# Lightning attention with mixture of depths: keys transposed into the state banks, wider compares, a reordered step

## The chip, the cores and the metric

The kernel runs on one core of one Trainium2 chip. The metric is the device time of one execution in microseconds (us). Five engines matter: TensorE (PE, with its weight loads listed apart as PEld), VectorE (DVE), ScalarE (ACT), GpSimd (POOL) and SyncE (SP), which issues loads. All data is fp32.

## The reference: what is computed

Attention with a decay per head is computed in blocks of 64 positions with a running state of 64 by 64 per head. Its output, with the heads side by side, is the input x of a layer in which a gate scores every row, and only the 128 best rows of each batch go through two matrix products.

```python
# q, k, v: (4, 8, 768, 64); lam: one decay per head
for b in range(nb):                                   # blocks of 64
    intra = np.einsum('bhic,bhjc->bhij', qb, kb) * Dmask[None]
    intra = np.einsum('bhij,bhjd->bhid', intra, vb)
    inter = np.einsum('bhid,bhde->bhie', qb * lam_pow[None], kv_state)
    out[:, :, sl] = intra + inter
    kb_dec = kb * rev_pow[None]
    kv_state = lam_block[None, :, None, None] * kv_state + np.einsum('bhsd,bhse->bhde', kb_dec, vb)
# x: (4, 768, 512), w1: (512, 1024), w2: (1024, 512), capacity 128
scores = np.einsum('bsd,d->bs', x, w_gate)
out = x.copy()
for b in range(B):
    top_idx = np.argpartition(-scores[b], capacity)[:capacity]
    xe = x[b, top_idx]
    h = np.maximum(xe @ w1, 0.0)
    ye = h @ w2
    g = 1.0 / (1.0 + np.exp(-scores[b, top_idx]))
    out[b, top_idx] = x[b, top_idx] + g[:, None] * ye
```

## The kernel before

The 4 x 768 rows are worked through in 24 tiles of 128 rows, g = 0 to 23, six for each batch. The program order is the order on each engine. A tile goes through these pieces (POOL multiplies, DVE masks and adds, ACT copies out of PSUM):

```python
def keys_decayed(g):        # POOL: kd = keys * powers of lam                      L184
def transposes(g, name, keep):
    t = loaded[g][0 if name == "qT" else 1]
    tp = bank([128, NHP, L], "tp_" + name)          # one of two PSUM banks, pm0 and pm1
    for hp in range(NHP):
        nc.tensor.transpose(tp[:, hp, :], in_=t[:, 2 * hp : 2 * hp + 2, :], identity=ident[:])
    dst = att.tile([128, NHP, L], FP32, name=name)
    nc.scalar.copy(out=dst[:], in_=tp[:])           # L199
    keep[g] = dst
def queries_decayed(g):     # POOL: qs = qT * powers of lam                         L204
def scores(g):              # PE: 16 small matmuls into po                          L217
def masked(g):              # DVE: p = scores * decay mask                          L224
def start_u(g):             # two PSUM tiles of one bank each, one buffer
    us[g] = [ps_u.tile([128, 512], FP32, name=f"pu{c}") for c in range(2)]
def state_products(g):      # PE: keys times values, columns 0 to 255 of pu0, pu1   L240
def decay_state(n):         # POOL: decayed = state * decay                         L250
def next_state(n):          # DVE: state = pu + decayed                             L261
def from_states(g):         # PE: qs times state, into po                           L271
def from_scores(g):         # PE: p times values, into po                           L282
def outputs(g):             # ACT: po to x_b, then one 256 KB store to out
def gate_scores(g):         # DVE: score of each row into sc                        L306
```

The rank of a row is the number of rows that beat it. The scores of a tile are spread along a row by a transpose, into columns 256 to 383 of a state tile, and compared with the scores of all tiles:

```python
def row(g, u, i=0):
    ...
    pb = us.pop(u)[i][:, 256 : 256 + L]
    nc.tensor.transpose(pb, in_=scs[b][:, t : t + 1].broadcast_to([128, 128]), identity=ident[:])   # L326
    nc.scalar.copy(out=rows_[b][:, t * L : (t + 1) * L], in_=pb)                                    # L329
    pbs[g] = pb

def compare(g):
    b, t = divmod(g, NT)
    sc, pb, beaten = scs[b], pbs.pop(g), beatens[b]
    # equal scores count where they stand earlier                                     L339
    nc.vector.scalar_tensor_tensor(out=cmp[:, :L], in0=pb, scalar=sc[:, t : t + 1], in1=not_before[:],
        op0=ALU.is_equal, op1=ALU.mult, accum_out=beaten[:, t, NT : NT + 1])
    for n in range(t):      # the earlier tiles against this one, from PSUM           L345
        nc.vector.tensor_scalar(out=cmp[:, :L], in0=pb, scalar1=sc[:, n : n + 1], ...,
            op0=ALU.is_gt, op1=ALU.add, accum_out=beaten[:, n, t : t + 1])
    # this tile against all up to it, from the copied row                             L350
    nc.vector.tensor_scalar(out=cmp[:, : (t + 1) * L], in0=rows_[b][:, : (t + 1) * L], ...,
        op0=ALU.is_ge, op1=ALU.add, accum_out=beaten[:, t, t : t + 1])
```

When a batch is complete, `ranks` (DVE) and `tokens` (PE, then DVE; L379, L388) make the list of 128 rows. `fetch` gathers them from `out` with an indirect DMA on POOL (L402), `gate` transposes them (L412), sixteen pieces do the products (eight `hidden`, L440, eight `back`, L454), and an indirect DMA scatters the result. The pieces are spread over the steps of the next batch. One step of the main loop:

```python
for g in range(NG):
    # loads for tile g + 6, one eighth of the weights in steps 4 to 11
    if g + 2 < NG:
        decay_state(2 * g + 4)
    for piece in early.pop(g, []):      # fetch, two steps after the end of a batch
        piece()
    from_scores(g)
    outputs(g)
    if g + 1 < NG:
        scores(g + 1); from_states(g + 1); masked(g + 1)
    start_u(g + 2)
    if g + 2 < NG:
        state_products(g + 2)
        next_state(2 * g + 4)
        decay_state(2 * g + 5)
    gate_scores(g)
    if g + 2 < NG:
        next_state(2 * g + 5)
    pieces = later.pop(g, [])
    starts = g in gates
    if starts:
        gates.pop(g)()
    if g + 2 < NG:
        transposes(g + 2, "qT", qTs)
        queries_decayed(g + 2)
    if g + 3 < NG:
        keys_decayed(g + 3)
    if starts and g > 0:
        row(g - 1, g + 2); compare(g - 1)
    in_order(pieces)
    if g + 2 < NG:
        transposes(g + 2, "kT", kTs)
    if not starts and g > 0 and NGR:
        row(g - 1, g + 2); compare(g - 1)
    if g in ranked:
        ranked.pop(g)()
    ...
```

Of the kernel before, what the change touches and what calls it, by code (L numbers as in the profile page):

```python
# [17 lines left out]
def kernel(  # L18
# [172 lines left out]
    def transposes(g, name, keep):  # L191
        t = loaded[g][0 if name == "qT" else 1]
        tp = bank([128, NHP, L], "tp_" + name)
        for hp in range(NHP):
            nc.tensor.transpose(  # L195
                tp[:, hp, :], in_=t[:, 2 * hp : 2 * hp + 2, :], identity=ident[:]
            )
        dst = att.tile([128, NHP, L], FP32, name=name)
        nc.scalar.copy(out=dst[:], in_=tp[:])  # L199
        keep[g] = dst  # L200
# [88 lines left out]
    def outputs(g):  # L289
# [7 lines left out]
        for c in range(2):  # L297
            nc.scalar.copy(out=x_b[half[c], t, :, 1, :], in_=po[half[1 - c], 1])  # L298
        nc.scalar.dma_start(
            out=out[b, t * L : (t + 1) * L, :], in_=x_b[:, t].rearrange("p a b e -> p (a b e)")  # L300
        )

# [13 lines left out]
    rows_, beatens, toks, pbs = {}, {}, {}, {}  # L316

    def row(g, u, i=0):

        b, t = divmod(g, NT)  # L320
        if t == 0:
# [3 lines left out]
        pb = us.pop(u)[i][:, 256 : 256 + L]  # L325
        nc.tensor.transpose(  # L326
            pb, in_=scs[b][:, t : t + 1].broadcast_to([128, 128]), identity=ident[:]
        )
        nc.scalar.copy(out=rows_[b][:, t * L : (t + 1) * L], in_=pb)  # L329
        pbs[g] = pb  # L330
# [3 lines left out]

    def compare(g):
        b, t = divmod(g, NT)
        sc, pb, beaten = scs[b], pbs.pop(g), beatens[b]
        cmp = mod.tile([128, S], BF16, name="cmp")
        nc.vector.scalar_tensor_tensor(  # L339
            out=cmp[:, :L], in0=pb, scalar=sc[:, t : t + 1], in1=not_before[:],  # L340
            op0=ALU.is_equal, op1=ALU.mult, accum_out=beaten[:, t, NT : NT + 1],
        )
        for n in range(t):
            cmp = mod.tile([128, S], BF16, name="cmp")
            nc.vector.tensor_scalar(  # L345
                out=cmp[:, :L], in0=pb, scalar1=sc[:, n : n + 1], scalar2=None,
                op0=ALU.is_gt, op1=ALU.add, accum_out=beaten[:, n, t : t + 1],
            )
        cmp = mod.tile([128, S], BF16, name="cmp")
# [124 lines left out]

    early, gates, later, ranked = {}, {}, {}, {}
    busy_until = [0]

    def put(step, key, piece):  # L480
# [74 lines left out]
    for g in range(NG):  # L555
# [4 lines left out]
        if g + 2 < NG:  # L560
            decay_state(2 * g + 4)
# [73 lines left out]
```

## Time and profile before

| | |
|---|---|
| median of 3 runs | 196.39 us (195.28 to 197.02) |
| the profiled execution | 194.65 us, span from first to last instruction 192.9 us |
| busy share of the span | PE 82%, PEld 65%, DVE 54%, POOL 51%, ACT 34% |
| moved by DMA | 32.26 MB, 80,964 packets, of which 75,680 under 512 bytes |
| mean granted TensorE clock | 0.973 |

The profile is one execution. Its page gives busy time by engine, the span in 40 slices, the DMA queues, the chain of work that ended last, the costliest groups of instructions, and the DMA issues. A row of a group or of a timeline names line, engine, operation, result and operands, and in brackets the idle time of the engine before it and what ended it; "issue" there means that the profile shows nothing the engine waited for. Matmuls overlap, so TensorE's busy share is not its share of full speed: an idle stretch on its timeline says more.

### The profile page before, as it was taken

To read this page: it belongs to the slowest core of one execution; us is meant where nothing else is said; L and a number is where in the kernel's file an instruction comes from. 1 tells how busy PE (TensorE), PEld (TensorE's weight loads), DVE (VectorE), ACT (ScalarE), POOL (GpSimd) and SP (SyncE) were. 2 spreads that over 40 slices of the span, in tenths; PEclk is the share of its full clock that TensorE was granted. 3 is DMA by queue.
4 is the path that set the end of the run, shared out by engine and by line. 5 is a ranking of instruction groups with operands and counts; after the bars stand their busy time and mean duration, and the time that the engine had idled before them with its cause. 6 is when DMAs were issued, how large, how long until landed. Compare 5 with 4: busy or idle time off the path is not lost.

```text
span 192.9 us, 8120 instructions
## 1 busy us (share of the span) xinstructions
PE 157.5 (82%) x3520; PEld 125.3 (65%) x3520; DVE 104.0 (54%) x393; ACT 66.1 (34%) x161; POOL 98.9 (51%) x110
## 2 busy tenths in 40 slices
PE   0896776969777399998888899989699899979980
PEld 0675665757666399896646689876467689439630
DVE  4824353667884653448664564754927678730010
ACT  2234333544443224533314353444234352111100
POOL 3486777476858641773556846458197410130002
PEclk9999998899999859999999999999999999999999
DMA  4999999998999999998999993110103211011001
GB/s 104 221 225 268 230 226 256 223 259 187 254 297 287 302 252 259 271 286 233 232 259 259 250 251 112 59 49 11 58 17 99 109 61 54 0 54 54 3 0 56
DMA packets 80964, 32.26 MB, mean 167 GB/s; under 512 B 75680, under 2 KB 75680, under 8 KB 80928
## 3 DMA queue, kind: packets, MB, share of 16 engines
q1 hardware_dynamic: 76688, 23.34, 54.2%
q10 hardware_dynamic: 3600, 6.30, 8.9%
q0 software_dynamic: 640, 2.10, 3.1%
q8 instruction: 28, 0.46, 0.9%
q14 instruction: 8, 0.07, 0.1%
HBM read 24.38 MB, written 7.34 MB: 164 GB/s over the span
## 4 chain that ended last, share of the span: by engine, by line
PE 51%; issue 16%; DVE 10%; POOL 9%; DMA 7%; ACT 4%; POOLq 1%; SPq 0%; ACTq 0%
PE ph L440 12%; PE py L454 11%; PE pu L240 5%; PE po L217 5%; PE po L271 5%; PE tp_qT L195 4%; PE tp_kT L195 4%; POOL qs L204 4%; DMA xs<-out_dram,tok 3%; PE po L282 3%; POOL kd L184 3%; POOL decayed L250 3%; DMA kn<-in_k_dram 3%; ACT kT L199 2%; DVE cmp L345 2%
## 5 line engine op out<-in xcount | busy, mean ns | idle before, releaser
L250 POOL TENSOR_TENSOR decayed<-state,decay 128x256 f32<-128x256 f32 x40 | 35.4, 884 | 39.0 <-DVE state L261 31.6
L204 POOL TENSOR_TENSOR qs<-qT,qpow 128x512 f32<-128x512 f32 x24 | 30.5, 1269 | 14.4 <-ACT qT L199 8.9
L440 PE MATMUL ph<-xsT,w_sb 128*128 128x128 f32 x256 | 32.6, 286 | 0.9 <-ACT xsT L416 0.7
L440 PEld LDWEIGHTS ph<-xsT,w_sb 128*128 128x128 f32 x256 | 31.2, 200 | 1.7 <-ACT xsT L416 1.5
L199 ACT COPY qT<-tp_qT 128x512 f32<-128x512 f32 x24 | 14.0, 584 | 50.0 <-PE tp_qT L195 46.8
L454 PE MATMUL py<-w_sb,hs 128*128 128x512 f32 x64 | 29.2, 596 | 0.0
L224 DVE TENSOR_TENSOR p<-po,mask 128x512 f32<-128x512 f32 x24 | 16.5, 689 | 19.2 <-PE po L271 19.2
L184 POOL TENSOR_TENSOR kd<-kn,kpow 128x512 f32<-128x512 f32 x24 | 25.1, 1044 | 3.2 <-DMA kn<-in_k_dram 3.1
L261 DVE TENSOR_TENSOR state<-pu,decayed 128x256 f32<-128x256 f32 x40 | 16.8, 421 | 16.9 <-POOL decayed L250 16.3
L240 PE MATMUL pu<-vn,kd 64*64 64x64 f32 x704 | 19.7, 229 | 7.3 <-issue 5.2
L240 PEld LDWEIGHTS pu<-vn,kd 64*64 64x64 f32 x704 | 16.1, 140 | 10.1 <-issue 7.0
L217 PE MATMUL po<-qT,kT 64*64 64x64 f32 x768 | 18.3, 228 | 5.0 <-issue 4.5
L271 PE MATMUL po<-state,qs 64*64 64x64 f32 x704 | 17.3, 225 | 5.9 <-POOL qs L204 3.0
L199 ACT COPY kT<-tp_kT 128x512 f32<-128x512 f32 x24 | 14.1, 587 | 23.3 <-PE tp_kT L195 23.3
L195 PE MATMUL tp_qT<-ident,qn 128*128 128x128 f32 x96 | 17.4, 309 | 5.1 <-DMA qn<-in_q_dram 5.1
L339 DVE SCALAR_TENSOR_TENSOR cmp<-pu,sc,not_before 128x128 bf16<-128x128 f32 x24 | 8.4, 349 | 23.8 <-ACT sc_row L329 17.0
L217 PEld LDWEIGHTS po<-qT,kT 64*64 64x64 f32 x768 | 14.5, 137 | 8.1 <-issue 5.4
L271 PEld LDWEIGHTS po<-state,qs 64*64 64x64 f32 x704 | 14.5, 138 | 7.1 <-POOL qs L204 3.7
L454 PEld LDWEIGHTS py<-w_sb,hs 128*128 128x128 f32 x64 | 11.5, 190 | 11.0 <-issue 11.0
L345 DVE TENSOR_SCALAR_CACHE_REDUCE cmp<-pu,sc 128x128 bf16<-128x128 f32 x60 | 17.8, 347 | 0.0
L298 ACT COPY x_b<-po 64x256 f32<-64x256 f32 x48 | 17.6, 366 | 0.6
L282 PE MATMUL po<-vn,p 64*64 64x64 f32 x768 | 16.8, 224 | 0.3 <-DVE p L224 0.3
(55 smaller groups left out, 170.6 us busy)
## 6 DMA issues: line engine op xcount, KB each, us to landing
qn<-in_q_dram SPq DMA_DIRECT2D x24, 256.0 KB, 5.3
kn<-in_k_dram SPq DMA_DIRECT2D x24, 256.0 KB, 5.5
vn<-in_v_dram SPq DMA_DIRECT2D x24, 256.0 KB, 6.0
out_dram<-x_b ACTq DMA_DIRECT2D x24, 256.0 KB, 3.6
w_sb<-in_moe_w_dram SPq DMA_DIRECT2D x8, 512.0 KB, 5.9
wg_b<-in_moe_w_gate_dram SPq DMA_DIRECT2D x1, 256.0 KB
xs<-out_dram,tok POOLq DMA_INDIRECT x4, 4.3
out_dram<-y,tok POOLq DMA_INDIRECT x4, 3.1
```

Of the source, the lines that this page charges most:

```text
L184: nc.gpsimd.tensor_tensor(out=kd[:], in0=loaded[g][1][:], in1=kpow[:].rearrange("p a b -> p (a b)").unsqueeze(2).broadcast_to([128, H, D]) ...
L195: nc.tensor.transpose(tp[:, hp, :], in_=t[:, 2 * hp : 2 * hp + 2, :], identity=ident[:])
L199: nc.scalar.copy(out=dst[:], in_=tp[:])
L204: nc.gpsimd.tensor_tensor(out=qs[:], in0=qTs[g][:], in1=qpow[:].rearrange("p a c i -> p a (c i)"), op=ALU.mult)
L217: nc.tensor.matmul(po[half[c], hh, 1, hp, :], lhsT=kT[half[hh], hp, half[c]], rhs=qT[half[hh], hp, half[c]], start=True, stop=True, skip_g ...
L240: nc.tensor.matmul(us[g][c][half[hh], hp * D : (hp + 1) * D], lhsT=kd[half[c], h, :], rhs=vn[half[c], h, :], start=True, stop=True, skip_g ...
L250: nc.gpsimd.tensor_tensor(out=t[:], in0=states[n][:], in1=decay[:], op=ALU.mult)
L271: nc.tensor.matmul(pos[g][half[hh ^ c], hh, 0, hp, :], lhsT=qs[half[hh], hp, half[c]], rhs=states[n][half[hh], hp, :], start=(hp == 0), st ...
L282: nc.tensor.matmul(pos[g][half[hh ^ c], hh, 0, hp, :], lhsT=p[half[c], hh, hp, :], rhs=vn[half[c], 2 * hp + hh, :], start=(hp == 0 and (2 ...
L345: nc.vector.tensor_scalar(out=cmp[:, :L], in0=pb, scalar1=sc[:, n : n + 1], scalar2=None, op0=ALU.is_gt, op1=ALU.add, accum_out=beaten[:, ...
L440: nc.tensor.matmul(ph[:, fc % 4, :], lhsT=w1_sb[:, dc, fc * 128 : (fc + 1) * 128], rhs=keep["xsT"][:, dc, :], start=(dc == 0), stop=(dc == ...
L454: nc.tensor.matmul(py[:], lhsT=keep["hs"][:, fc, :], rhs=w2_sb[:, fc, :], start=(fc == 0), stop=(fc == NFC - 1),)
```

## The change

It does seven things.

1. The transposed keys no longer take one of the two shared banks: they go into columns 256 to 511 of the two state tiles, two pairs of heads in each, directly behind the transposed queries. ACT copies them out in two halves.
2. The row of scores takes a shared bank. Only the compare for equality reads it there; all others read the row that ACT has copied to SBUF, and several are put together: earlier tiles are compared with two or three later ones at once, after tiles 2, 4 and 5 of a batch.
3. The equality compare stands before the second state of the step, the other compares after it.
4. The decayed keys stand at the head of the step, and the decayed queries ahead of the decay of the second state on POOL.
5. The rows of an expert are fetched in the step before, behind the list of rows; the ranks come ahead of the list, in the same step.
6. The six stores of the second batch are held back and written as two stores of three tiles in steps 12 and 13.
7. In the last steps, one expert piece instead of two is in step 23, so that five pieces instead of four stand behind the last fetch.

The core of the diff:

```diff
-    def transposes(g, name, keep):
-        t = loaded[g][0 if name == "qT" else 1]
-        tp = bank([128, NHP, L], "tp_" + name)
...
+    def transposes(g):
+        tq = bank([128, NHP, L], "tq")
+        tk = [u[:, NHP * D :].rearrange("p (a i) -> p a i", i=L) for u in us[g]]
+        W = NHP // 2
+        for i, dst in ((0, tq), (1, None)):
+            for hp in range(NHP):
+                nc.tensor.transpose(
+                    dst[:, hp, :] if i == 0 else tk[hp // W][:, hp % W, :],
+                    in_=loaded[g][i][:, 2 * hp : 2 * hp + 2, :], identity=ident[:],
+                )
+        qT = att.tile([128, NHP, L], FP32, name="qT")
+        nc.scalar.copy(out=qT[:], in_=tq[:])
+        kT = att.tile([128, NHP, L], FP32, name="kT")
+        for i in range(2):
+            nc.scalar.copy(out=kT[:, i * W : (i + 1) * W, :], in_=tk[i])
...
+        if b == 1 and B > 2:
+            kept.append(t)
+        else:
+            store(b, t, t + 1)
...
-        pb = us.pop(u)[i][:, 256 : 256 + L]
+        pb = bank([128, L], "pb")
...                                              # row: transpose, copy, equality compare
+    def count_later(b, groups, last):
+        for t in groups:
+            if upto[b][t] < last:
+                cols = slice((upto[b][t] + 1) * L, (last + 1) * L)
+                count(b, t, cols, ALU.is_gt, last)
+                upto[b][t] = last
     def compare(g):
...
+        first = upto[b].pop(NT + t, 0)
+        count(b, t, slice(first * L, (t + 1) * L), ALU.is_ge, t)
+        if t == NT // 2 - 1 or t == NT - 1 or (b == B - 1 and t == NT - 2):
+            count_later(b, range(t), t)
+        elif t == NT - 2:
+            count_later(b, range(NT // 3), t)
+    def compare_older(g):
+        b, t = divmod(g, NT)
+        if t > 0:
+            count(b, t, slice(0, t * L), ALU.is_ge, 0)
+            upto[b][NT + t] = t
...
-            early.setdefault(s + 2, []).append(fetch)
+            put(s + 1, 6, fetch)
...
-            counts = [2, 3, 3, 3, 3, 2] if whole else [1, 1, 2]
+            counts = [2, 3, 3, 3, 3, 2] if whole else [1, 1, 1]
...
     for g in range(NG):
...
+        if g >= 2 * NT and kept:
+            store_kept()
         if g + 2 < NG:
             decay_state(2 * g + 4)
-        for piece in early.pop(g, []):
-            piece()
+        if g + 3 < NG:
+            keys_decayed(g + 3)
         from_scores(g)
         outputs(g)
         if g + 1 < NG:
             scores(g + 1)
             from_states(g + 1)
             masked(g + 1)
-        start_u(g + 2)
+        if g in ranked:
+            ranked.pop(g)()
+        if g % NT == 0 and g > 0 and NGR:
+            compare_older(g - 1)
         if g + 2 < NG:
+            start_u(g + 2)
             state_products(g + 2)
+        if g in gates:
+            gates.pop(g)()
+        if g + 2 < NG:
+            transposes(g + 2)
+            queries_decayed(g + 2)
             next_state(2 * g + 4)
             decay_state(2 * g + 5)
         gate_scores(g)
...                                              # step 22 takes the rows of tiles 21 and 22, step 23 none
+        if g % NT == 0:
+            for r in rows:
+                row(r)
+        else:
+            in_order(pieces)
+            for r in rows:
+                row(r)
         if g + 2 < NG:
             next_state(2 * g + 5)
...
+        for r in rows:
+            compare(r)
+        if g % NT == 0:
+            in_order(pieces)
```

## The prediction

> **What bounds the kernel now.** A step g is one pass of the main loop; it begins with the matmuls of line 282. I first cut the span at steps where the work changes, in the table of busy time by stretch (span, PE, weight loads, DVE, ACT, POOL, TensorE clock, DMA share, GB/s):
>
> ```profile
> 13.18:61.76 48.58, 36.47 (x1207) 30.75 (x1207) 29.64 (x106) 19.82 (x51) 34.54 (x37) 0.96 1.00 247
> 61.76:73.58 11.82, 8.78 (x143) 8.13 (x142) 5.62 (x25) 3.40 (x10) 6.28 (x7) 0.71 1.10 280
> 73.58:157.52 83.94, 76.24 (x1858) 61.12 (x1858) 50.06 (x186) 34.44 (x84) 47.97 (x49) 1.00 0.61 159
> 157.52:187.50 29.98, 28.59 (x189) 19.68 (x188) 10.72 (x49) 4.87 (x12) 1.98 (x2) 1.00 0.09 33
> ```
>
> Four stages: attention alone (steps 0 to 8, 5.4 us each), step 9 (11.8 us), attention with the experts (steps 10 to 22, 6.5 us each), and the last experts, where TensorE hardly idles. The reader is to see that no engine is full in the first stage, while the DMA share is 1.00.
>
> Then I read TensorE's timeline in the first stage, at the rows where it idles:
>
> ```profile
> 16.47 0.33 PE L271 MATMUL po<-state,qs 64*64 64x64 f32 x4 [1.68 <-issue]
> ...
> 32.09 0.34 PE L217 MATMUL po<-qT,kT 64*64 64x64 f32 x1 [1.73 <-issue]
> ...
> 43.08 0.34 PE L217 MATMUL po<-qT,kT 64*64 64x64 f32 x7 [1.70 <-issue]
> ...
> 52.32 0.39 PE L217 MATMUL po<-qT,kT 64*64 64x64 f32 x11 [0.83 <-issue]
> ```
>
> The gaps lie inside a run of equal matmuls, where nothing else is waited for. The part on DMA queues has a queue for the program itself:
>
> ```profile
> q8 instruction: 28, 0.46, 0.9%
> ```
>
> That is 16,384 bytes a packet. I numbered TensorE's instructions (four for an fp32 matmul, two for a transpose, one for a separate wait; 7128 in all): every gap of this kind lies 256 instructions after the last. In the trace's packet records these packets begin at 14.10, 19.27, 24.06, 29.52, 34.95, 40.85, 44.42, 49.46, 54.49 and 59.83 us, last about 1 us, and TensorE executes the first instruction of each block 1.27 to 1.63 us after its packet ended, ten times out of ten, up to 62.26 us. Later it does so 2.0 to 7.3 us after. So up to step 9 the kernel is bound by the arrival of its own instructions: nine blocks from 16.47 to 62.26 us, 5.09 us each.
>
> In the later stages the rows with idle time are these:
>
> ```profile
> 67.61 1.08 PE L412 MATMUL pt<-ident,xs 128*128 128x128 f32 x4 [1.75 <-DMA xs<-out_dram,tok]
> ...
> 88.59 0.69 PE L240 MATMUL pu<-vn,kd 64*64 64x64 f32 x32 [0.54 <-issue]
> ...
> 95.53 0.69 PE L240 MATMUL pu<-vn,kd 64*64 64x64 f32 x32 [0.81 <-issue]
> ...
> 97.64 0.30 PE L379 MATMUL pk<-ids,hit 128*128 128x2 bf16 x6 [0.83 <-DVE hit L368]
> ```
>
> The state products of line 240 start at 88.59 and 95.53, and the last narrow compare out of their PSUM tile (line 345) has just been read then. The page calls it "issue", but it is the tile coming free.
>
> [...] The trace has no difference at 128 columns (347 ns from PSUM, 344 ns from the copied row), but a fixed cost of about 0.2 us is seen: 128, 256 and 384 columns take 344, 476 and 610 ns. [...] The decay multiplies (line 250) agree: 0.72 to 0.74 us mostly, 1.10 us beside line 306, which reads two SBUF tensors.
>
> **The change, part by part.**
>
> *Compares and keys.* Scores go into their own bank and keys into the upper halves of the state tiles, so the state products no longer wait for compares. Per batch, before: 15 narrow compares at a pitch of 0.27 us. After: nine of 128 to 384 columns from the copied row, about 3.2 us instead of 4.1, plus one more compare for the last tile. VectorE saves some 0.8 us a batch and is not the bound. What counts is TensorE: the waits 0.26, 0.54, 0.81 us in steps 11 to 13, and again in 17 to 19 (0.26, 0.54, 0.81), 3.2 us in all.
>
> *A step of TensorE without waits*, from the rows of step 11 and 12: lines 282, 217 and 271 0.64, 0.64 and 0.47, line 240 0.55, queries 0.50, keys 0.44, experts 2.68 (24 matmuls of L440) or 2.58 (six of L454), score row 0.2: 6.0 to 6.1 us. Steps 10 to 22 gain against that: 0, 0.5, 0.7, 1.4, 0.5, 1.0, 0, 0.6, 0.7, 1.4, 0.5, 1.5, and -0.4 in step 22, whose own score row now waits for the gate. In these I leave 0.45 us for the ranks in steps 13 and 19 (ranks now follow the mask: hits ready some 3.7 us into the step, TensorE there at 3.25), and 0.5 us in four steps where an indirect DMA of POOL stands beside a gap inside line 240. Sum 8.4. In steps 10 and 11 TensorE would now use up 256 instructions in 4.0 us, under the 5.09 of a fetch while loads still fill the queues: 1.4 us given back. Net 7.0 us.
>
> *Earlier fetch.* xs is asked for in step 7 instead of 8, some 5 us sooner, while it takes 6.5 us to land. The 1.75 us wait goes, and with it the half clock of 66 to 73 us, in which 16 matmuls took 3.4 us instead of 1.8. Step 9 then has about 5.5 to 6 us of work against 11.8; the fetch limit lets it end at about 69.3 us where the kernel before began step 10 at 73.6.
>
> *Decayed queries ahead of the second state, and six held-back stores.* The first takes 0.6 to 1.0 us waits for qs (line 271) out of the steps; the second takes 256 KB of writes out of each of steps 6 to 11 and writes two times 768 KB in steps 12 and 13. Both help in a stage bound by instruction blocks, so I count only 37 instructions fewer (about 0.4 us by step 9) and a little for the lighter queues.
>
> *Start.* Keys share a tile with the state products, so the first products wait for the key copies, and the second keys for the second state, at 11.97 us. The first scores move from 10.88 to about 12.5; I count 1.2 us lost, and it shifts the first block.
>
> Together: step 10 begins 4.4 us earlier (start, fewer waits and step 9 netted), the dense steps give 7.0, and the last expert's 0.69 us wait for xs goes, since five pieces instead of four stand behind the fetch. 4.4 + 7.0 + 0.7 = 12.1 us: 196.4 - 12.1 = 184.3. I say 185, because the fetch may collide more than I count.
>
> **Rivals.** *The loop over POOL is the bound, not the blocks.* Queries behind the decay, then lines 271, 240, state, decay: 1.27 + 0.64 + 0.55 + 0.45 + 1.1 and latencies, 4.2 us, and the stalls add to it. The change breaks that loop; steps 0 to 8 would drop to some 4.7 us, and the time to about 180. For it: POOL waits 31.6 us for states. Against: ten blocks out of ten began right behind their packet. *New waits replace the old.* The second state now stands behind the equality compare, which waits for the score row behind 2.7 us of expert work, and one more tile fights for two banks; TensorE would still wait at the state products, and only step 9 gains: about 192. Against: that state ends some 0.9 us into the next step, and its products start 1.75 us into it. *The gathered stores collide* with the fetch of the second batch: POOL is held, TensorE two or three microseconds idle in steps 13 to 15: about 187.
>
> **Range and chances.** The centre is 185; 181.5 if the POOL loop counts for a part, 190 if a third of the dense gain is eaten by new waits or block arrivals. Over 2% faster means under 192.5, which needs only step 9 and none of the rest: 0.95. Within 2%: 0.04. Slower: 0.01.
>
> **What would show it.** Right: first products later (first line-282 row at 14.3 to 15 us); gaps inside matmul runs, 256 instructions apart, still about 5 us apart up to step 9; no wait for xs in step 9; no gaps ahead of the state products from step 11 on; step 22 with a wait for its score row. Wrong: steps 0 to 8 under 4.9 us (the loop was the bound), or a new wait on ACT or DVE ahead of keys, queries or score rows in the dense steps. A half-clock stretch elsewhere would cost 1 to 3 us.

## The result, and the profile after

The change takes 188.09 us (median of 4 executions, 187.14 to 189.73) against 195.83 us (median of 4, 194.19 to 197.02): ratio 0.962, 95% interval 0.951 to 0.972. I had said 185.0, range 181.5 to 190. A profile is one execution: the one of the kernel before spans 192.9 us, near the quick end of its times, the one of the change 188.0 us, its longest of four. So the profiles differ by 4.9 us where the medians differ by 7.7. In the experiments the ratios leave out executions more than 1.5% above the fastest of their kernel, the medians do not, and the profiles marked * are of such executions.

The table of busy time by stretch, cut at the same steps as before (columns: span, PE, weight loads, DVE, ACT, POOL, TensorE clock, DMA share, GB/s):

```profile
15.66:66.34 50.68, 36.64 (x1208) 32.00 (x1206) 31.44 (x94) 20.85 (x61) 35.70 (x37) 0.91 1.02 244
66.34:72.42 6.08, 6.08 (x142) 5.81 (x141) 4.92 (x13) 3.18 (x10) 4.20 (x5) 0.88 1.11 254
72.42:153.77 81.35, 73.78 (x1860) 60.83 (x1859) 56.61 (x180) 35.18 (x98) 51.45 (x50) 0.98 0.67 175
153.77:188.00 34.23, 28.37 (x188) 19.67 (x187) 10.56 (x42) 4.82 (x11) 3.17 (x3) 0.99 0.09 31
```

Against the table of the kernel before: the start is 2.48 us longer (15.66 for 13.18), steps 0 to 8 take 2.10 us more (50.68 for 48.58), step 9 takes 5.74 less (6.08 for 11.82), steps 10 to 22 take 2.59 less (81.35 for 83.94), and the rest 1.2 less (34.23 for the 35.4 left of 192.9). Of the two large gains that were predicted, only step 9 came at its size.

Where TensorE waited between 15 and 72 us, first the kernel before, then the change (columns: sum in us, times, longest):

```profile
PE po L217 <- issue: 4.5, 4, 1.7
PE po L271 <- POOL qs L204: 3.0, 4, 1.0
PE po L271 <- issue: 2.9, 3, 1.7
PE pt L412 <- DMA xs<-out_dram,tok: 1.7, 1, 1.7
...
PE pk L379 <- DVE hit L368: 0.7, 1, 0.7
```

```profile
PE po L278 <- issue: 3.2, 2, 2.0
PE pu L247 <- DVE state L268: 2.8, 3, 1.2
PE po L224 <- issue: 2.8, 2, 1.6
PE pk L417 <- DVE hit L406: 2.5, 1, 2.5
PE po L278 <- POOL qs L211: 2.4, 4, 1.3
```

The wait for xs is gone. In its place stand 2.5 us of waiting for the hits, 0.7 before, and 2.8 us for VectorE's states, for which TensorE did not wait before. The waits inside equal matmuls ("issue") fell from 7.4 to 6.0 us. The program's queue moved one packet less:

```profile
q8 instruction: 27, 0.44, 1.0%
```

Numbered as in the prediction, 6 of the 10 blocks that start before 72 us now run within 1.75 us of their packet's end; before it was 10 of 10. From 19.64 to 67.16 us they are 5.28 us apart on average (5.09 before). So blocks no longer hold every step.

In the dense steps no row shows a gap ahead of the state products any more up to step 20, as predicted. These gaps are left (TensorE's timeline):

```profile
81.27 0.60 PE L198 MATMUL tq<-ident,qn 128*128 128x128 f32 x4 [0.71 <-issue]
...
93.96 0.50 PE L278 MATMUL po<-state,qs 64*64 64x64 f32 x17 [1.22 <-issue]
...
107.54 0.51 PE L224 MATMUL po<-qT,kT 64*64 64x64 f32 x19 [2.18 <-issue]
...
153.51 0.32 PE L349 MATMUL pb<-ident,sc 128*128 128x128 f32 x1 [1.45 <-DVE cmp L355]
```

The first three lie at block starts, 1.30 to 1.49 us after the packet's end: the shorter steps of the change run into the block limit here too. The last is step 22.

**The wait that I had not seen.** VectorE's waits between 15 and 72 us, the kernel before and then the change:

```profile
DVE state L261 <- POOL decayed L250: 7.7, 9, 2.3
...
DVE state L261 <- PE pu L240: 0.6, 2, 0.3
```

```profile
DVE state L268 <- ACT kT L206: 9.5, 6, 2.5
...
DVE state L268 <- POOL decayed L257: 3.2, 7, 0.8
...
DVE state L266 <- ACT kT L206: 1.3, 1, 1.3
```

The state of a tile waits for ScalarE's key copies, which it does not use. One step of each shows it (lines 259 and 266 make the first state of a batch, lines 261 and 268 the others); first the kernel before, then the change (columns: start, duration, then the idle time before it and what ended it):

```profile
38.27 0.69 PE L240 MATMUL pu<-vn,kd 64*64 64x64 f32 x32 [0.30 <-POOL kd L184]
...
39.01 0.42 DVE L259 COPY state<-pu 128x256 f32<-128x256 f32 x1 [0.28 <-PE pu L240]
...
39.58 1.05 POOL L250 TENSOR_TENSOR decayed<-state,decay 128x256 f32<-128x256 f32 x1 [1.37 <-DVE state L259]
```

```profile
39.66 0.65 PE L247 MATMUL pu<-vn,kd 64*64 64x64 f32 x32
...
41.47 0.65 ACT L206 COPY kT<-pu 128x256 f32<-128x256 f32 x2
41.65 1.28 POOL L211 TENSOR_TENSOR qs<-qT,qpow 128x512 f32<-128x512 f32 x1 [1.55 <-ACT qT L203]
41.88 0.42 DVE L266 COPY state<-pu 128x256 f32<-128x256 f32 x1 [1.28 <-ACT kT L206]
...
42.88 1.18 POOL L257 TENSOR_TENSOR decayed<-state,decay 128x256 f32<-128x256 f32 x1
```

Before, the state starts 0.05 us after its products end (38.96); after, 1.57 us (40.31 to 41.88). It reads columns 0 to 255 of a bank whose columns 256 to 511 hold the keys. In the trace the state waits for the semaphore that ScalarE's copies raise: the state of this row, which reads the first of the two banks, starts 0.03 us after that bank's copy (41.85 us), while the copy of the second bank still runs (to 42.12 us). Whether that order was made because both stand in one tile or because they stand in one bank, no run here tells. In all, seven states wait 10.8 us for key copies (9.5 at line 268, 1.3 at line 266), while the waits for POOL's decays fall from 7.7 to 3.2 us. So the part of the change that moves the keys lengthens the loop from state to state, in the row shown by some 1.5 us. The new order on POOL, queries ahead of the second decay, fills that time: qs starts at 41.65, before the state is even there.

### The profile page after: what moved, and what is told of

Read it like the earlier page. It is cut to its first block, busy times and chain, and to the rows that moved or that the text cites. A ratio compares the mean times of both kernels' runs of the same rounds, so it can differ in the third digit from the quotient of the medians.

```text
span 188.0 us, 8090 instructions
## 1 busy us (share of the span) xinstructions
PE 153.5 (82%) x3520; PEld 124.9 (66%) x3520; DVE 110.6 (59%) x357; ACT 68.0 (36%) x185; POOL 103.4 (55%) x110
## 2 busy tenths in 40 slices
DMA packets 80898, 32.23 MB, mean 171 GB/s; under 512 B 75616, under 2 KB 75616, under 8 KB 80864
## 4 chain that ended last, share of the span: by engine, by line
PE 56%; issue 16%; POOL 10%; DVE 9%; DMA 3%; ACT 3%; POOLq 1%; ACTq 0%; DVEq 0%
PE ph L478 11%; PE py L492 10%; PE pu L247 7%; PE tq L198 6%; PE po L289 6%; POOL qs L211 6%; PE po L278 5%; PE po L224 5%; PE pu L198 3%; POOL decayed L257 3%; ACT qT L203 3%; DMA lam_b<-in_lam_dram 2%; DVE cmp L365 2%; DMA out_dram<-y,tok 2%; DVE state L268 1%
## 5 line engine op out<-in xcount | busy, mean ns | idle before, releaser
L257 POOL TENSOR_TENSOR decayed<-state,decay 128x256 f32<-128x256 f32 x40 | 37.1, 927 | 16.7 <-DVE state L268 13.8
L478 PE MATMUL ph<-xsT,w_sb 128*128 128x128 f32 x256 | 31.1, 278 | 0.7 <-ACT xsT L454 0.7
L478 PEld LDWEIGHTS ph<-xsT,w_sb 128*128 128x128 f32 x256 | 29.8, 193 | 1.1 <-ACT xsT L454 0.9
L365 DVE TENSOR_SCALAR_CACHE_REDUCE cmp<-sc_row,sc 128x128 bf16<-128x128 f32 (+3 forms) x66 | 29.9, 497 | 0.0
L203 ACT COPY qT<-tq 128x512 f32<-128x512 f32 x24 | 14.0, 585 | 42.6 <-PE tq L198 41.4
L328 DVE CUSTOM_DVE_ANT_0 xg<-x_b,wg_b 128x512 f32<-128x512 f32 x24 | 25.9, 1077 | 0.0
L198 PE MATMUL tq<-ident,qn 128*128 128x128 f32 x96 | 17.8, 315 | 5.6 <-DMA qn<-in_q_dram 4.9
L247 PEld LDWEIGHTS pu<-vn,kd 64*64 64x64 f32 x704 | 17.7, 147 | 4.7 <-DVE state L268 1.8
L492 PEld LDWEIGHTS py<-w_sb,hs 128*128 128x128 f32 x64 | 11.4, 190 | 11.9 <-issue 10.8
L289 PEld LDWEIGHTS po<-vn,p 64*64 64x64 f32 x768 | 14.5, 144 | 7.0 <-issue 4.2
L198 PE MATMUL pu<-ident,kn 128*128 128x128 f32 x96 | 17.1, 305 | 2.0 <-DVE state L268 1.9
```

The source lines that it names most:

```text
L198: nc.tensor.transpose(dst[:, hp, :] if i == 0 else tk[hp // W][:, hp % W, :], in_=loaded[g][i][:, 2 * hp : 2 * hp + 2, :], identity=ident[:],)
L247: nc.tensor.matmul(us[g][c][half[hh], hp * D : (hp + 1) * D], lhsT=kd[half[c], h, :], rhs=vn[half[c], h, :], start=True, stop=True, skip_g ...
L257: nc.gpsimd.tensor_tensor(out=t[:], in0=states[n][:], in1=decay[:], op=ALU.mult)
L289: nc.tensor.matmul(pos[g][half[hh ^ c], hh, 0, hp, :], lhsT=p[half[c], hh, hp, :], rhs=vn[half[c], 2 * hp + hh, :], start=(hp == 0 and (2 ...
L328: nc.vector.tensor_tensor_reduce(out=xg[:], in0=x_bs[b][:, t].rearrange("p a b e -> p (a b e)"), in1=wg_b[:], scale=1.0, scalar=0.0, op0=A ...
L365: nc.vector.tensor_scalar(out=cmp[:, : cols.stop - cols.start], in0=rows_[b][:, cols], scalar1=scs[b][:, t : t + 1], scalar2=None, op0=op, ...
```

## The experiments

All of the twelve were timed beside the kernel before. The profiles' step starts (first matmul of the p times values group), in us:

```
                                   step 1  step 7  step 10  step 23  end    steps 10 to 22
kernel before                      18.25   50.20   73.58    157.52   192.9  83.94
change                             22.56   51.99   72.42    153.77   188.0  81.35
change, every tile stored at once  20.80   52.31   73.19    150.21   184.4  77.02
change, ranks at step end          21.98   53.44   73.08    151.34   185.6  78.26
change, queries after decay        22.96   56.14   77.91    157.36   191.6  79.45
change, 2 KB load packets          22.10   54.26   74.74    151.21   185.5  76.47
change, fewer instructions         21.24   51.82   71.76    149.44   183.7  77.68
change, loads left out             21.09   55.66   74.71    149.93   185.6  75.22
change, keys in own bank to 10     19.01   49.74   72.17    150.37   184.6  78.20
change, keys in own bank to 1 *    20.33   49.48   71.62    152.87   187.1  81.25
change, POOL's order of before *   21.28   60.81   86.57    170.20   204.4  83.63
change, late gather *              23.12   52.85   74.01    154.78   189.0  80.77
before, queries early              18.23   52.84   75.23    159.49   194.7  84.26
before, fetch early                18.11   49.09   72.35    158.14   193.3  85.79
```

### Queries behind the second decay again

```
-            queries_decayed(g + 2)
             next_state(2 * g + 4)
             decay_state(2 * g + 5)
+            queries_decayed(g + 2)
```

> The change, with the decayed queries again behind the second decay on POOL, as before. Theory (steps 0 to 8 are bound by instruction blocks, so POOL's order is worth little there; in the dense steps TensorE waits 0.6 to 1.0 us for qs where POOL comes late): steps 0 to 6 change by less than 0.2 us each, the time grows by 0 to 2 us. Rival (the loop over POOL is the bound and this order is what the change gained by): each of steps 1 to 8 grows by 0.5 us or more, the time by 5 us or more.

Measured: 196.85 us, ratio 0.998 (0.994 to 1.003). The whole gain is gone: the medians are 8.8 us apart, the ratios (0.998 and 0.962) some 7 us. TensorE's waits between 15 and 72 us:

```profile
PE po L278 <- POOL qs L211: 11.3, 8, 2.2
PE po L278 <- issue: 2.4, 1, 2.4
```

My theory fell. Waits for qs rose from 2.4 to 11.3 us, and step 10 begins at 77.91 instead of 72.42, while steps 10 to 22 keep their gain (79.45 us against 83.94). The change's other parts win in the dense steps what they lose in the first stage; the order on POOL takes the loss away.

### The same order alone, on the kernel before

```
             state_products(g + 2)
+            transposes(g + 2, "qT", qTs)
+            queries_decayed(g + 2)
             next_state(2 * g + 4)
             decay_state(2 * g + 5)
```

(and the two lines taken out further down)

> The kernel before, with one part of the change alone: queries transposed and decayed right behind the state products, ahead of the second decay. Theory of two limits: in the kernel before blocks arrive 5.09 us apart whatever POOL does, so steps 0 to 8 gain only where a wait for qs stands beside no block, 0 to 2 us in all, and the time is 194 to 196. Rival (POOL's loop is the bound, and this order is what the change gains by, as the 8.8 us lost with the order undone suggest): steps 1 to 8 take 4.7 us in the mean instead of 5.4, the time is 187 to 191.

Measured: 197.48 us, ratio 1.017 (1.008 to 1.026): slower by 0.8 to 2.6%, outside both expectations. TensorE's waits between 15 and 72 us:

```profile
PE po L271 <- issue: 4.1, 4, 1.2
PE po L217 <- issue: 4.0, 3, 2.0
PE pu L240 <- DVE cmp L345: 3.7, 3, 1.7
PE po L271 <- POOL qs L204: 1.2, 4, 0.7
```

The waits for qs fell (3.0 to 1.2 us), but the waits at blocks did not (7.4 to 8.1), and 9 of 10 blocks still run right behind their packet; 3.7 us of waits for the narrow compares came on top, and VectorE waits 18.7 us for POOL's decays (7.7 before), of which the second now stands behind the queries. So the order is worth nothing by itself on the kernel before. Beside which other part of the change it pays (keys in the state banks, the moved compares, decayed keys at the head of a step), no run separates.

### POOL's whole order of before

```
-        if g + 3 < NG:
-            keys_decayed(g + 3)      # ahead of from_scores
...
             next_state(2 * g + 4)
             decay_state(2 * g + 5)
+            queries_decayed(g + 2)
+        if g + 3 < NG:
+            keys_decayed(g + 3)
```

> The change, with POOL's order as it was before in full: first decay, second decay, queries, and the keys of the next tile last (with only the queries put back the keys stood ahead of the second decay, an order that neither kernel has). Theory (the queries ahead of the second decay are what the change gains by, once its other parts have taken the compares out of the way): the time stays near that of the run with the queries put back, 193 to 197, and TensorE waits 1 to 2 us for qs in steps 1 to 9. Rival (the 8.8 us lost there came from the keys standing between the two decays): 187 to 190, and the waits for qs are under 0.7 us.

Measured: 205.36 us, ratio 1.035 (1.023 to 1.048), outside both expectations. The rival is refuted: the keys between the two decays were not the cost. With the keys last as well, the ratio rises by another 0.037, some 7 us. So without its order on POOL the change is slower than the kernel before. TensorE waits 10.9 us for qs between 15 and 72 us, no more than with the queries alone put back (11.3); why it is so much slower stays open.

### The earlier gather: alone on the kernel before, and taken out of the change

```
-            early.setdefault(s + 2, []).append(fetch)
+            put(s + 1, 6, fetch)
```

> The kernel before, with one part of the change alone: the gather of the chosen rows is issued in steps 7, 13 and 19 behind the tokens, and not in steps 8, 14 and 20. Theory (step 9 as predicted): the 1.75 us wait for xs and the half clock of 66 to 73 us go, step 9 takes 6 to 7 us instead of 11.8, and the time falls by 4 to 6 us, to 190 to 192. Rival (step 9 would then wait for the weights or for a block, or the half clock comes elsewhere): step 9 takes 8 us or more, the time falls by less than 2 us.

Measured: 194.18 us, ratio 0.999 (0.995 to 1.003): nothing. In the profile step 9 takes 6.59 us instead of 11.82, as the theory had it, and steps 7 and 8 together 16.67 instead of 11.56. In TensorE's timeline the two rows with new gaps:

```profile
53.99 0.59 PE L217 MATMUL po<-qT,kT 64*64 64x64 f32 x11 [3.60 <-issue]
...
63.11 0.69 PE L240 MATMUL pu<-vn,kd 64*64 64x64 f32 x32 [2.58 <-DVE cmp L339]
```

The first is a block whose packet started 5.2 us after the block before it began to run. It lies ahead of the gather, which POOL issues at 61.35 us, so the gather did not cause it. The second does come from the gather: VectorE's compare of line 339 waits 3.88 us for a small POOL instruction that now stands behind it. So of the 5.1 us only some 2.6 are shown to be a wait that was moved. The other way round, the change with the late gather and with the ranks at the end of a step:

> The change, with the gather of the chosen rows issued two steps after a batch, as before, and the ranks at the end of a step, as before. Theory of the prediction (the earlier gather is worth about 5 us in step 9): step 9 takes 10 us or more, 4 us of it with a wait for xs and half clock, and the time is 191 to 193. Rival (the earlier gather only moves the wait: on the kernel before, alone, it made step 9 5.2 us shorter and steps 7 and 8 5.1 us longer): steps 7 to 9 together take 20 to 22 us as in the change, and the time is 187 to 189.

Measured: 189.23 us, ratio 0.966 (0.960 to 0.972), against 0.962 for the change: a loss of some 1 us, which the intervals do not separate. Step 9 takes 9.67 us, with a block gap of 2.37 us and half clock from 67.6 us but no wait for xs, and steps 7 to 9 together 21.16 us (20.44 in the change). The rival holds, within 0.3 us of its time: the gather's place is not worth 5 us here.

### Ranks at the end of a step

```
-        if g in ranked:
-            ranked.pop(g)()          # behind the next mask
...
         if g % NT == 0:
             in_order(pieces)
+        if g in ranked:
+            ranked.pop(g)()
```

> The change, with the ranks and hits worked out at the end of steps 6, 12 and 18 as before, not behind the next mask. Theory (VectorE itself is late in step 7, 7.39 us busy of 7.76, by the gathered wide compares and by two-input operations beside POOL): the wait of TensorE for hits falls from 2.46 us by no more than the 0.6 us of a mask, the mask comes 1.2 to 1.6 us later and takes the gain back; the time stays within 1 us of the change. Rival (the place of the ranks behind the mask is the cause): the wait falls under 0.5 us, step 7 takes 5.7 us instead of 7.8, and the half clock of 61.0 to 67.8 us goes with it: 2 to 4 us faster than the change.

Measured: 187.07 us, ratio 0.959 (0.953 to 0.966), no different from the change. TensorE still idles 2.45 us for the hits, though step 7 is 0.22 us shorter; the half clock of 61.0 to 67.8 us is gone from this profile all the same. So the place of the ranks is not the cause of the wait; the theory, that VectorE itself is late, fits. Its rows in step 7, first two of the kernel before, then the change:

```profile
49.62 0.68 DVE L306 CUSTOM_DVE_ANT_0 xg<-x_b,wg_b 128x512 f32<-128x512 f32 x1
...
54.17 0.96 DVE L368 TENSOR_TENSOR hit<-rank,token 128x768 bf16<-128x768 f32 x1
```

```profile
51.81 0.87 DVE L365 TENSOR_SCALAR_CACHE_REDUCE cmp<-sc_row,sc 128x640 bf16<-128x640 f32 x1
...
52.94 1.15 DVE L328 CUSTOM_DVE_ANT_0 xg<-x_b,wg_b 128x512 f32<-128x512 f32 x1
...
57.04 0.69 DVE L231 TENSOR_TENSOR p<-po,mask 128x512 f32<-128x512 f32 x1
...
57.87 1.43 DVE L406 TENSOR_TENSOR hit<-rank,token 128x768 bf16<-128x768 f32 x1
```

The 640 column compare now stands ahead of the first state, the mask ahead of the ranks, and two operations are longer than in the kernel before (gate 1.15 for 0.68 us, hit 1.43 for 0.96), both begun while POOL works on qs (52.27 to 53.55 and 57.21 to 58.48 us). The two profiles show such pairs throughout. Of the change's 24 operations of line 328 the 18 that start some 0.6 us into a multiply for qs take 1.15 to 1.43 us, the other six 0.68 to 0.76; of the kernel before's 40 decays on POOL (line 250) the 17 that start beside line 306 take 1.04 to 1.11 us, the other 23, some of them beside compares or the mask, 0.71 to 0.75. Lines 328, 306 and 406 each read two SBUF tensors. 0.8 + 0.6 + 0.5 + 0.5 is 2.4 us, about the wait; but of these only the mask's part was tried, so the sum is not shown.

### Fewer TensorE instructions in tiles 0 to 9

```
-            if n % (2 * NT) == 0:
+            if n % (2 * NT) == 0 or (hp >= 2 and g <= 9):
                 continue
```

It leaves half of the state part of the outputs out.

> The change without half of the state part of the outputs (line 278, head pairs 2 and 3) in tiles 0 to 9: it leaves 72 matmuls, 288 TensorE instructions and some 2.1 us of TensorE work out, and nothing of the other engines. Theory of the prediction (blocks alone, 5.09 us for 256): step 10 begins 5.7 us earlier than in the change, at 66.7. Theory of two limits: a step without a block's start already takes 4.2 to 4.7 us and is held by POOL, so only the steps with a gap gain, 0.3 us a step: step 10 begins 1.5 to 3 us earlier, the rows marked issue become rarer, and the wait of step 7 for hits stays. Rival (POOL's loop alone): step 10 moves by less than 1 us.

Measured: 185.36 us, ratio 0.955 (0.948 to 0.962). Step 10 begins 0.66 us earlier than in the change, not 5.7 and not 1.5 us: by that mark the rival, POOL's loop, is the nearest, though it was not the whole bound of the kernel before. Only 2 of 9 blocks now run right behind their packet, steps 1 to 6 take 5.10 us in the mean (4.90 in the change), and the time went here instead (TensorE's waits, 15 to 72 us):

```profile
PE pu L247 <- DVE state L268: 6.6, 7, 1.1
PE pk L417 <- DVE hit L406: 2.5, 1, 2.5
```

With fewer blocks in the way the state loop holds the steps, at about the same height (VectorE waits 14.2 us for key copies, 10.8 in the change).

### Packets of 2 KB

```
+            whole = src[b].rearrange("h s d -> (h s) d")
+            at = slice(c * L * H, (c + 1) * L * H)
-            nc.sync.dma_start(out=t[:], in_=src[b, :, rows, :].rearrange("h p d -> p h d"))
+            nc.sync.dma_start(out=t[:], in_=whole[at, :].rearrange("(p h) d -> p h d", h=H))
```

> The change, with every load of queries, keys and values read as one stretch of 256 KB (2 KB packets in place of 256 byte ones). Rows and heads are then mixed up: it computes with wrong rows, but moves the same bytes with the same instructions. Theory of two limits (instruction blocks that wait behind the load packets, and POOL with some 4.2 us of work a step): blocks arrive sooner than every 5 us, the gaps inside equal matmuls in steps 0 to 6 nearly go, steps 1 to 6 take 4.2 to 4.6 us instead of 4.9 in the mean, no less, and step 10 begins 2 to 4 us earlier than at 72.4. Theory of the prediction (blocks alone): steps fall to 3.5 to 4 us, step 10 begins 8 us or more earlier. Rival (the loop over POOL alone, or a delay of the blocks that has nothing to do with the load packets): blocks as late as before or of no effect, step 10 within 1 us.

Measured: 188.92 us, ratio 0.973 (0.966 to 0.980). In the first stage 9 of 10 blocks run right behind their packet, whose start is 2.1 to 4.5 us after the block before began (1.2 to 3.0 in the change). Steps 1 to 6 take 5.36 us in the mean, and step 10 begins 2.32 us later than in the change. Small packets are not what delays the blocks.

### Loads of tiles 6 to 23 left out

```
+        if g >= AHEAD:
+            loaded[g] = first[g % AHEAD]
+            return
```

> The change without the loads of tiles 6 to 23: they are computed from the tiles 0 to 5 already held, so it leaves 13.5 MB of loads out and has wrong data, but the same instructions on all engines but SP. Theory (the instruction blocks are late because they stand behind loads in the DMA queues): in steps 1 to 9 a block's packet starts within 1.5 us of the first instruction of the block before it, at most 3 of 10 blocks run within 1.75 us of their packet's end, steps 1 to 6 take 4.2 to 4.6 us in the mean, and step 10 begins 2 to 4 us earlier than at 72.4. Rival (the delay of some 5 us a block is the fetch's own, as 2 KB load packets, which did not shorten it, suggest): 6 or more of 10 run right behind their packet, and steps 1 to 6 take 4.8 us or more.

Measured: 186.10 us, ratio 0.950 (0.944 to 0.956), with 18.06 MB moved instead of 32.23. Neither expectation fits the whole first stage, because the weights came early and filled the queues up to 42 us. Two stretches of it:

```profile
25.00:35.00 10.00, 7.11 (x240) 5.95 (x228) 6.08 (x17) 4.63 (x14) 7.72 (x9) 1.00 0.99 319
...
45.00:55.00 10.00, 7.70 (x262) 6.67 (x261) 7.39 (x22) 4.83 (x15) 8.06 (x8) 0.99 0.09 30
```

Up to 42 us (DMA share 0.99) the packets start 1.7 to 5.0 us after the block before began, and five of five blocks run within 1.7 us of their packet's end. From there to 76 us (share 0.09) they start 0.1 to 1.2 us after, and TensorE has no gap marked issue. So within this run blocks come late while the queues are full and early once they are empty. But steps 5 to 7, with no block late, take 4.76, 5.40 and 7.50 us, against 5.18, 5.44 and 7.76 in the change. TensorE's waits from 45 to 72 us:

```profile
PE pu L252 <- DVE state L273: 3.0, 4, 0.9
PE pk L422 <- DVE hit L411: 2.5, 1, 2.5
```

### Every tile stored at once

```
-        if b == 1 and B > 2:
-            kept.append(t)
-        else:
-            store(b, t, t + 1)
+        store(b, t, t + 1)
```

> The change, with every tile of the second batch stored at once, as before, instead of two stores of 768 KB in steps 12 and 13. Theory (the gathered stores stand ahead of instruction blocks: in the change a block's packet starts 5.1, 3.2 and 4.7 us after the first instruction of the block before it ran, and TensorE idles 1.22 and 2.18 us inside equal matmuls in steps 13 and 15): these gaps fall under 0.7 us each, steps 12 to 15 take 26 us instead of 28.9, steps 6 to 11 lose at most 1 us, the end comes 1 to 3 us earlier, 185 to 187. Rival (the blocks are late in steps 12 to 15 because a step has become shorter and uses up 256 instructions faster, whatever is stored): the gaps stay, and the time stays within 1 us of 188 or grows by the store traffic in steps 6 to 11.

Measured: 187.31 us, ratio 0.962 (0.956 to 0.969), the same as the change. In its profile the gaps in steps 13 and 15 are gone or smaller (none, and 0.77 us) and steps 12 to 15 take 25.07 us instead of 28.90. But of the other runs of the change, which keep the gathered stores, eight have these steps at 23.8 to 26.8 us and one (keys of tiles 0 and 1 in their own bank) at 29.2, so the long ones of the change's profile are not shown to come from the stores. Step 9 takes 7.94 us here, with 1.5 us of it a wait for weights.

### Keys of the first tiles in a bank of their own

```
         W = NHP // 2
+        if g < 2:                    # second run: g < 11
+            own = bank([128, NHP, L], "tk")
+            tk = [own[:, i * W : (i + 1) * W, :] for i in range(2)]
+        else:
+            tk = [u[:, NHP * D :].rearrange("p (a i) -> p a i", i=L) for u in us[g]]
```

> The change, with the keys of tiles 0 and 1 alone transposed into a bank of their own, as before. Theory (the start was mis-sized: I counted 1.2 us, the first row of line 289 came 2.48 us later and that of step 1 4.31 us later, because the first keys wait 1.95 us for the second state and the first instruction block is asked for later): the 1.95 us wait goes, step 0 begins at 13 to 14 us instead of 15.66, step 1 at 18 to 19.5 instead of 22.56, and the end comes 2 to 3 us earlier than in the change, about 185.5. Rival (the block arrivals after it absorb a shorter start, or the late start is only the half clock of 20.0 to 23.4 us): step 1 moves by less than 1 us and the end stays within 1 us of 188.

Measured with tiles 0 and 1: 186.35 us, ratio 0.955 (0.949 to 0.962), 1.7 us under the change, though the intervals overlap. The 1.95 us wait is gone and step 0 begins at 13.19 us, as in the theory; step 1 begins at 20.33, between the theory and the rival. Only 3 of 10 blocks run right behind their packet here, and yet steps 1 to 6 take 4.86 us in the mean (4.90 in the change): with the keys of the later tiles still in the state banks, the loop holds most of these steps (VectorE waits 10.5 us for key copies). So the same was done for every tile of the first stage:

> The change, with the keys of tiles 0 to 10 transposed into a bank of their own, as before, and those of tiles 11 to 23 in the state banks; all else as in the change. Theory (keys in the state bank make the first state of a tile wait for ACT's key copies: VectorE idles 9.5 us for them between 15 and 72 us in the change, and that loop, not the instruction blocks alone, holds steps 1 to 8): this wait goes, the state products no longer stand 0.4 to 1.2 us behind VectorE's states, steps 1 to 6 take 4.3 to 4.6 us in the mean instead of 4.9, the start gains 1 to 2 us as with tiles 0 and 1 alone, and the time is 182 to 185. Rival (blocks of 256 instructions some 5 us apart hold these steps whatever the loop does): the wait for key copies goes, steps 1 to 6 stay at 4.8 to 5.0 us with the gaps inside equal matmuls in its place, and the time is that of the run with tiles 0 and 1 alone, 185 to 187.

Measured with tiles 0 to 10: 185.16 us (183.82 to 186.60), ratio 0.945 (0.939 to 0.951). It is faster than the change, whose quickest execution took 187.14, and has the lowest median of all with the reference's whole work. TensorE's waits between 15 and 72 us:

```profile
PE po L282 <- issue: 4.6, 6, 2.3
PE ph L482 <- DMA w_sb<-in_moe_w_dram: 3.0, 1, 3.0
PE pk L421 <- DVE hit L410: 2.5, 1, 2.5
...
PE po L228 <- issue: 1.3, 2, 0.9
```

VectorE's waits in the same stretch:

```profile
DVE state L272 <- POOL decayed L261: 8.3, 7, 2.0
...
DVE state L272 <- ACT kT L210: 0.5, 1, 0.5
```

VectorE's wait for key copies fell from 10.8 to 0.5 us, that for POOL's decays rose from 3.2 to 8.3, and the state products' wait for states fell from 2.8 to 0.8. Steps 1 to 6 take 5.12 us in the mean (4.90 in the change), 8 of 10 blocks run right behind their packet: the rival was right about these steps, and the time lies in its range too. The start is back (first row at 13.36 us, step 1 at 19.01 instead of 22.56). But step 10 begins at 72.17, 0.25 us before that of the change, because step 9 now waits 3.0 us for weights. In the profiles the rest of the difference lies in steps 10 to 22, where the two kernels have the same program; where the 2.9 us between the medians come from is not settled.

## Why the prediction was right, and which terms were mis-sized

**The time** was in the range, 3 us above the centre: of the 12.1 us summed, 7.7 came (4.9 between the profiles). That it stayed in the range was in part luck. A cost that I had not seen, key copies in the loop of states, and a gain that I had counted as next to nothing, the order on POOL, nearly cancelled in steps 0 to 8; with the queries back behind the second decay the change takes 196.85 us, outside the range.

**Blocks bound steps 0 to 8.** Right for the kernel before: 10 of 10 blocks, and its two variants 9 and 8 of 10. What I left out is that a second limit, the loop of states over VectorE and POOL, stands at nearly the same height. Where instructions are left out, or blocks come sooner, the loop holds the steps (5.10 us in the mean of steps 1 to 6 with fewer instructions, 4.86 with the keys of tiles 0 and 1 in their own bank); where key copies are out of the loop, the blocks hold them (5.12). No run takes both away at once, so that there is no third limit at this height is not shown. This is why the first stage got no shorter, and why rival A was neither right nor wrong: the loop was not *the* bound, but it was no slack either.

**"Both help in a stage bound by instruction blocks, so I count only 37 instructions fewer."** This failed. Queries ahead of the second decay are worth some 7 us in the change (ratio 0.998 without, 0.962 with) and less than nothing in the kernel before (1.017). I had counted the shared tile of keys and state products only at the start ("the first products wait for the key copies"); it also makes states wait for key copies, seven times between 15 and 72 us.

**Start, 1.2 us lost.** Mis-sized: 2.48 us at step 0 (15.66, past the 14.3 to 15 us that I had given as a sign), and 4.3 at step 1, since the first block starts later too (19.64 for 16.47 us) and the clock is half for longer: the records have full clock from 16.59 us, then half from 20.0 to 23.4, where the kernel before had full clock from 11.68 to 32.2 (a 64 by 64 matmul takes 311 ns ahead of these starts and at half clock, 218 at full). Keys in their own bank bring the first row back to 13.36, with full clock from 13.04.

**Step 9 at 5.5 to 6 us, step 10 at 69.3.** Step 9 was nearly right: 6.08. But on the kernel before the same early gather brought no time, so its size in one profile is not its worth. Step 10 began at 72.42, in part because of the start, and because I left out the step where the hits are needed first: step 7 waits 2.46 us for them and steps 7 and 8 together take 2.8 us more than before. I had left 0.45 us for the ranks in steps 13 and 19 (measured 0.39 and 0.77) and nothing in step 7. The net 4.4 us measured 1.16.

**Dense steps, 7.0 us.** 2.59 us in the profile of the change. In the runs with all the work of the reference and the new order on POOL it is 2.7 (keys of tiles 0 and 1 in their own bank), 3.2 (late gather), 5.7 (ranks at step end), 5.7 (keys to tile 10) and 6.9 (every tile stored at once): 7.0 is the upper end. The rows agree with the mechanism: no waits ahead of the state products in steps 11 to 19. But the moved compares were not tried alone, so what they bring in time is not shown. In the change's profile block gaps of 1.22 and 2.18 us and a half clock from 108.8 to 112.2 us cost steps 13 and 15 what is missing: predicted gains 1.4 and 1.0, measured 0.16 and -2.55. The 1.4 us for block stalls, put into steps 10 and 11 alone, were too small. Step 22 lost 1.50 instead of 0.4, 1.45 of it the wait for the equality compare.

**The last expert, 0.7 us.** Right: the 0.69 us wait for xs is gone there.

**Rivals.** New waits did replace old ones (key copies, hits, step 22), but not at the state products of the dense steps. That gathered stores collide was not shown.

## What to carry to other kernels

Before counting what a removed wait brings, look for the second limit: here two stood within a few tenths of a microsecond a step, so that easing either alone left the first stage as long as it was, and one part of the change, worth nothing on the kernel before, was worth some 7 us beside the others. When data moves into a tile that another engine reads, follow every reader of that tile through the whole loop, not only the first time: here seven states waited 10.8 us for copies that they do not use. A change that is meant to move one transfer is to be judged over all the steps from its issue to its use: with the early gather on the kernel before, step 9 gained 5.2 us and steps 7 and 8 lost 5.1, of which 2.6 lay behind the gather itself.

## What the runs showed of the hardware that was not expected

- In the run without the loads of tiles 6 to 23, an instruction block's packet starts 1.7 to 5.0 us after the block before it began to run while the DMA queues are full (share 0.99), and 0.1 to 1.2 us after when they are nearly empty (0.09). With full queues the other runs have mostly 1.2 to 5.2 us up to step 9, with 256 byte and 2 KB packets alike, but some packets start sooner (five of the ten with the keys of tiles 0 and 1 in their own bank, at -0.2 to 1.2 us). So full queues do not always delay a block.
- Half clock came in stretches of 3.41 us or twice that (20.0 to 23.4, 61.0 to 67.8 and 108.8 to 112.2 us in the change). The records give a clock of 0.50 in these, and stretches at 1.00 that are multiples of the same length: 37.55 and 40.96 us in the change, 11 and 12 times 3.41; 20.48 and 30.72 us in the kernel before, 6 and 9 times. In the 3.41 us ahead of each of the three drops TensorE idled 1.8 to 2.2 us in one gap. A gap of that size is not always followed by half clock: with the ranks at the end of a step the wait for hits is as long as in the change (2.46 us there), but the records have full clock from 18.65 to 182.49 us.

```profile
60.38 0.30 PE L417 MATMUL pk<-ids,hit 128*128 128x2 bf16 x6 [2.45 <-DVE hit L406]
```

  The time at full clock in all 14 profiles, cut into stretches of 3.41 us from the edges of the clock records, sorts them by their idle time: all 23 stretches with 1.96 us or more of TensorE idle time were followed by half clock, 19 of 55 with 1.37 to 1.87 us, and none with less. The gap shown crosses an edge at 59.61 us, with 1.70 us idle in the stretch before it, which is among the idle times that half clock followed in some stretches only. So it fits that where a gap falls counts too.
- A VectorE read of one half of a PSUM tile (one bank) was made to wait for ScalarE's read of the other half, and started 1.57 us after its own data was complete; with the keys in a bank of their own such waits fell from 10.8 to 0.5 us.
